# Respacing the weight preparation of the second mixture: sums through the first mixture, splits through the experts

## The chip, the cores and the metric

One core of one Trainium2 chip runs the whole program. The metric is the device time of one execution in microseconds; the kernel before takes 1052.43 us (median of 3 runs, 1051.04 to 1053.65). All other times here are of one execution that the hardware profiler took: 1052.22 us in all, of which 1050.6 us lie between its first and its last instruction (the span).

## The reference

Three stages follow each other, all in float32.

1. Linear attention over 4 batches, 8 heads, 576 positions: features exp(+p) and exp(-p) of projections of q and k, sums of k-features times v, a quotient.
2. A first mixture over the 2304 tokens (512 wide): `h = max(x @ w1, x @ w2, x @ w3)` with 768 hidden columns, then `h @ w_out`.
3. A second mixture with 8 experts: noisy logits choose two experts for each token, and `out[token] += weight * (relu(x @ w1[e]) @ w2[e])`, 1024 hidden columns in each expert.

The kernel writes each operand of most products as a high part (rounded) and a low part (the rest); such a product takes three matmuls, high by high, high by low, low by high.

## The kernel before, in words

**Order.** The kernel writes its order out by hand. `Plan.at(t, f, ...)` records a step with a due time; at the end all steps are sorted by due time and called in that order. The instructions of TensorE (PE), ScalarE (ACT), VectorE (DVE) and SyncE (SP, which issues the direct DMAs) stand in their queues in just that order (`tc.manual_schedule` names these four engines). Each queue is worked off in order and as soon as its waits allow: a due time decides who stands before whom and holds nobody back. GpSimd (POOL) is not in that list. The framework orders its queue by itself; only the routing scatters are tied by hand (`in_order`) to come after the POOL instruction that was recorded before them. The due times of PE's work come from a running `clock[0]`, which `pe(dur, ...)` advances by planned durations: 1.92 us for a group of 12 matmuls with 384 columns (`G1`) and for 9 with 512 columns (`G2`).

**First mixture.** The tokens go through in 6 chunks of 384. A chunk has 6 hidden blocks f. Each has three groups `first(c, f, j)` into three rotating PSUM banks `s`. `larger` frees them: ACT copies the bank of j = 0 into `a`, DVE takes the maximum with the banks of j = 1 and 2 (line 775 and 777). `hidden` splits `a` (ACT writes hh, DVE hl, lines 126 and 127), and `second(c, f)` (line 794) multiplies that by the output weights. Counted in planned us from the start of a chunk (c from 1 to 4; a chunk is 49.08 long): the last `second` of the chunk before stands at 1.92; `second` of block 0 to 4 at 16.44, 24.12, 31.80, 39.48 and 47.16; each has its block's next three groups behind it. `larger` of block 3, j = 0 stands at 28.01, j = 2 at 31.85; the split of the next chunk's input, `split_x`, at 32.30 and `hidden` of block 3 at 32.40; `larger` of block 4, j = 0 at 35.69; `hidden` of block 5 at 47.76. The routing of the chunk before runs beside: its ACT and DVE steps lie at 14.6 to 21.2, and at 22.2 come six scatters on POOL (line 944), each an indirect DMA of `mt` rows to `meta`. `mt` has two buffers, and POOL fills them with token numbers (lines 866 and 867).

**Weight sums.** The experts 2 to 7 (the units with seven products) use a seven-product scheme for the first layer, which needs sums and differences of weight quarters. They are made during the first mixture, in 24 jobs, written out of SBUF into a DRAM tile `sums`, high and low part, and read back much later. A job has four steps: `quarter_load` (SP, two DMAs into a `raw` tile, line 1259), `quarter_sum` (four adds on POOL, lines 1267 to 1270), `quarter_high` (ACT writes `qh`, line 1274), `quarter_out` (DVE writes the low part back into `raw`, line 1279, and SP stores both, line 1281). There are two `raw` tiles in the whole kernel and one `qh` buffer. Six jobs lie in each of the chunks 1 to 4, at 8 + 5.51 i: the third job of a chunk has its load at 19.0, sum at 24.0, high at 27.7, out at 29.2.

**Experts.** A unit is one expert's tokens: unit 0 is expert 0's first 512, unit 1 the next 128 of expert 0, unit n from 2 on expert n - 1 (608 tokens). Units 3 to 8 take the seven products (`seven(n)`). The weights come through a ring of 12 slots, each with a high and a low tile. `refill(i, n, wait)` fetches slots as they come free: `w2_load` (SP into `raw`), `w2_high` (ACT, line 1289), `w2_low` (DVE, line 1297), each at least 3.0 us after the last, `w2_low` 1.2 us behind `w2_high`. A slot that holds a ready sum is loaded from `sums` by two DMAs (line 1292). In unit n `refill` is called after the first layer and after the second. In planned us a unit with seven products takes 21.28 for the first layer and about 28 for the second; unit 2 takes 24.3 and about 28.

The lines of the plan that the change touches:

```python
t = max(clock[0] + wait, split_at[-1] + 3.0)
at(max(split_at[-2] + 0.01, t - 9.0), w2_load, en, en, j)
at(t, w2_high, en, j)
at(t + 1.2, w2_low, en, j)
```

Of the kernel before, what the change touches and what calls it, by code (L numbers as in the profile page):

```python
# [23 lines left out]
class Plan:  # L24
# [5 lines left out]
    def at(self, t, f, *x):  # L30
        self.ops.append((t, len(self.ops), f, x))
# [7 lines left out]
def tile_linear_attention__then__moe__then__noisy_top2_moe(  # L39
# [27 lines left out]
    KD = DM // P  # L67
    F1 = FF1 // P
    F2 = FF2 // P
# [7 lines left out]
    NCHUNK = NT // CT  # L77
# [13 lines left out]
    at = plan.at  # L91
# [967 lines left out]
    ORDER7 = (1, 6, 7, 4, 5, 3, 2)  # L1059

    def seven(n):
        return isinstance(n, int) and n > SEVEN
# [166 lines left out]
    def summed(key, i):  # L1229
        return isinstance(key, int) and key >= SEVEN and i < len(ORDER7) and SEVENTHS[ORDER7[i]][0] == "S"  # L1230
# [68 lines left out]
    def overflow_table():  # L1299
# [12 lines left out]
                "wgn": wgn[one].rearrange("p k e -> p (k e)"),  # L1312
                "cmp": tp.tile([1, MAXO * NREG], F32, name="cmp")}
        used = dict.fromkeys(room, 0)

        def tt(where, *shape):
# [73 lines left out]
    G1 = 3 * KD * CW / 2400   # L1390
    G2 = 3 * CT * DM / 2400
    clock = [T]

    def pe(dur, f, *x):
        at(clock[0], f, *x)
        clock[0] += dur

    def after(d, f, *x):
        at(clock[0] + d, f, *x)

    def first_pe(c, f, j):
        pe(G1, first, c, f, j)
        after(0.05, larger, j)
        if j == 2:
            after(0.6, hidden, c, f)
# [33 lines left out]
    for i in range(2 * 4):  # L1439
        g, j = 1 + i // 4, i % 4  # L1440
        t = END + 0.1 + i * 3.2
# [3 lines left out]
    def finish(c):  # L1445

        for t in range(CT):
            after(0.05 + 0.5 * t, x2_out, c, t)

    def tail(c, i):  # L1450
        if i == 0:
            for t in range(2):
                pe(0.45, x2_turn, c, t)
                after(0.0, x2_in, c, t)
            if c < NCHUNK - 1:
                after(0.1, begin_route, c)
        elif i == 1:
            pe(0.45, x2_turn, c, 2)
            after(0.0, x2_in, c, 2)
        elif i == 2:  # L1460
            pe(1.3, gates, c)
            after(0.0, gates_out, c)
        else:
            pe(0.35, gates_turn, c)
            route_at(c, clock[0])

    split_at = [0.0, 0.0]

    pairs = [(e, j) for e in range(E)
             for j in range(F2 // 2 + (KD if e < SEVEN else len(ORDER7)))]  # L1470

    def base(e):
        return 12 + pairs.index((e, 0))

    def room(i):

        if i < len(pairs):
            after(0.9, w2_room, *pairs[i], i + 12)
            if summed(*pairs[i]):
                after(1.0, w2_high, *pairs[i])  # L1480

    def refill(i, n, wait=0.1, rooms=True):
        for i in range(i, i + n):
            if i >= len(pairs):
                return
            if rooms:
                after(0.0, w2_room, *pairs[i], i + 12)
            if summed(*pairs[i]):
                if rooms:
                    after(1.0, w2_high, *pairs[i])  # L1490
                continue
            en, j = pairs[i]
            t = max(clock[0] + wait, split_at[-1] + 3.0)
            at(max(split_at[-2] + 0.01, t - 9.0), w2_load, en, en, j)
            at(t, w2_high, en, j)
            at(t + 1.2, w2_low, en, j)
            split_at.append(t)

    units = [(0, cap_a, 0), (0, cap_b, E * REGION)] + [(e, cap, e * REGION) for e in range(1, E)]
    jobs = [(e, a, c) for e in range(SEVEN, E) for a in range(2) for c in range(2)]  # L1500
    for c in range(NCHUNK):
        if 0 < c < NCHUNK - 1:
            pitch = (F1 * (3 * G1 + G2) - 13.0) / 6
            for i, job in enumerate(jobs[6 * (c - 1):6 * c]):
                t = clock[0] + 8.0 + pitch * i
                at(t, quarter_load, *job)
                at(t + 5.0, quarter_sum, *job)
                at(t + 8.7, quarter_high, *job)
                at(t + 10.2, quarter_out, *job)
        if c == NCHUNK - 1:  # L1510
            split_at.append(clock[0] + 25.0)
        for f in range(F1):
            for j in range(3):
                if c or f or j > 1:
                    first_pe(c, f, j)
                if c and f == 0 and j == 0:
                    pe(G2, second, c - 1, F1 - 1)
                    finish(c - 1)

                if c and 1 <= 3 * f + j < 5:  # L1520
                    tail(c - 1, 3 * f + j - 1)
            if f in (3, 4) and c + 1 < NCHUNK:
                after(0.5, split_x, c + 1, f - 3)
            if c == NCHUNK - 1 and f == F1 - 1:
                break
            if f:
                pe(G2, second, c, f - 1)
            if c == NCHUNK - 1 and f % 2 == 1:
                refill(2 * f - 2, 3)
            if c == NCHUNK - 1 and f and f % 2 == 0:  # L1530
                refill(2 * f - 1, 1)
    c = NCHUNK - 1
# [12 lines left out]
    finish(c)  # L1545
    split_at.append(clock[0] + 19.0)
    refill(8, 4)

    def open_experts():
# [8 lines left out]
    after(-0.01, open_eh)  # L1558

    for n, (e, M, row0) in enumerate(units):  # L1560
        nsp = 1 if M <= 512 else 2
        cw = M // nsp
        nxt = n + 1 < len(units)
# [5 lines left out]
        if seven(n):  # L1569
            for two in ((0, 1), (2, 3)):  # L1570
                for q_ in ORDER7:
                    for f in two:
                        pe(2 * 3 * HN / 2400, product, n, e, q_, f)
                        d0, d = (-0.03, 0.01) if two[0] and q_ == ORDER7[-1] else (0.02, 0.44)
                        after(d0, sum7, n, q_, f)
                        if q_ in PART7:
                            after(d0 + d, relu7, n, q_, f)
                            after(d0 + 2 * d, low7, n, q_, f)
                    if two[0]:
                        room(base(e) + ORDER7.index(q_))  # L1580
        elif M > P:
            for f in range(F2):
                for s in range(nsp):
                    if n == 0:
                        for i in range(2):
                            pe(d1 / 2, expert1, n, e, M, f, s, cw, range(2 * i, 2 * i + 2))
                            if f < 2:
                                tail(NCHUNK - 1, 2 * f + i)
                    else:
                        pe(d1, expert1, n, e, M, f, s, cw)  # L1590
                    after(0.0, expert_hidden, n, f, s, cw)
                if n == 0 and f == 1:
                    after(0.0, open_experts)
                    tp = clock[0] + 0.01
        else:
            for a in range(2):
                pe(2.56, tile1, n, e, a)
                after(0.0, tile_relu, n, a)
        if seven(n):
            refill(base(e), len(ORDER7), 2.5, False)  # L1600
        elif n:
            refill(base(e), KD, 3.0 if n == 1 else 0.1)
        if n == 4:
# [68 lines left out]
                        turns7(4)  # L1672
                        rows7(2)
        if n:
            refill(base(e) + (len(ORDER7) if seven(n) else KD), F2 // 2)

    ET = mybir.EngineType
    with tc.manual_schedule(engines={ET.PE, ET.Activation, ET.DVE, ET.SP}):
# [55 lines left out]
```

## Time and profile before

| | |
|---|---|
| median of 3 runs | 1052.43 us |
| the profiled execution | 1052.22 us |
| its span | 1050.6 us |
| PE busy (matmul) | 992.9 us, 95% |
| DVE, ACT, POOL busy | 591.3, 448.6, 484.3 us |
| mean granted TensorE clock | 0.978 |
| HBM traffic | 160 GB/s over the span |

Matmuls overlap in the profile, so 95% busy does not mean that nothing can be gained by packing them; but a gap of PE is a gap. The granted clock is the share of full speed (2.4 GHz) that TensorE got in a stretch; it has two levels, 1.0 and 0.5.

In a row of a timeline the columns are: start in us, duration in us, engine, line of the kernel, operation, tiles written and read, shapes, count, and in brackets the idle time of that engine before it and what ended that.

### The profile page before, as it was taken

The page shows a single profiled execution, that of the slowest core. Times are in us where ns is not written, and L with a number is a line of the kernel's source. Part 1 is how long each engine was busy: PE and PEld are TensorE (multiplying, and loading weights), DVE is VectorE, ACT ScalarE, POOL GpSimd, SP SyncE. Part 2 cuts the span into 40 slices and gives each one's busy share as a digit, 9 for nine tenths or more (in the row PEclk, how much of TensorE's full clock was granted, in tenths as well). Part 3 has the DMA queues.
Part 4 walks back from the last instruction along what each step waited for, and adds up shares of the span by engine and source line. Part 5 has one row for each costly group of instructions (what it writes and reads, how often), then busy time and mean ns, then how long its engine had stood idle before and what let it go on. Part 6 is the DMA issues. An engine that isn't in the chain of part 4 may idle for free. (4 is left out here: it accounts for less than half of the span.)

```text
span 1050.6 us, 17138 instructions
## 1 busy us (share of the span) xinstructions
PE 992.9 (95%) x6285; PEld 867.5 (83%) x6285; DVE 591.3 (56%) x1272; ACT 448.6 (43%) x879; POOL 484.3 (46%) x553
## 2 busy tenths in 40 slices
PE   9999999999979978789799999899999999999995
PEld 7777777789978978789689778889888998989893
DVE  5888888874343434434335544365758666666630
ACT  6666666633323224223233523334545464546330
POOL 2677555670243352524404253235556464646261
PEclk9999999999989999899899999999999999999998
DMA  7547765252256353463634443554848393938211
GB/s 192 158 139 182 211 194 169 83 158 64 90 155 216 101 181 131 141 207 84 200 132 121 141 118 126 211 195 145 289 126 303 104 331 104 321 120 315 85 53 43
DMA packets 125351, 169.07 MB, mean 161 GB/s; under 512 B 35630, under 2 KB 86958, under 8 KB 125266
## 3 DMA queue, kind: packets, MB, share of 16 engines
q1 hardware_dynamic: 114338, 138.35, 42.5%
q0 software_dynamic: 10928, 29.62, 8.2%
q8 instruction: 50, 0.82, 0.3%
q14 instruction: 35, 0.29, 0.1%
HBM read 119.38 MB, written 49.14 MB: 160 GB/s over the span
## 5 line engine op out<-in xcount | busy, mean ns | idle before, releaser
L767 PE MATMUL s<-xh,wh 128*128 128x384 f32 x432 | 151.8, 351 | 25.2 <-ACT a L775 25.0
L767 PE MATMUL s<-xl,wh 128*128 128x384 f32 x432 | 148.4, 344 | 0.0
L767 PE MATMUL s<-xh,wl 128*128 128x384 f32 x432 | 148.0, 343 | 0.0
L1225 POOL DMA_INDIRECT out_dram<-o,emeta x40 | 48.1, 1203 | 133.5 <-DVE o L1223 81.1
L767 PEld LDWEIGHTS s<-xh,wh 128*128 128x128 f32 x432 | 83.9, 194 | 30.1 <-ACT a L775 26.7
L1289 ACT ACTIVATE wh<-raw 128x1024 fp32r<-128x1024 f32 x58 | 61.3, 1057 | 61.6 <-DMA raw<-in_moe_w_dram 42.5
L1215 PE MATMUL p<-wh,hh 128*128 128x512 f32 (+1 forms) x216 | 86.4, 400 | 0.0
L1297 DVE TENSOR_TENSOR wl<-raw,wh 128x1024 fp32r<-128x1024 f32 x58 | 70.8, 1220 | 26.6 <-ACT wh L1289 26.6
L1215 PE MATMUL p<-wh,hl 128*128 128x512 f32 (+1 forms) x216 | 85.3, 395 | 0.0
L1215 PE MATMUL p<-wl,hh 128*128 128x512 f32 (+1 forms) x216 | 85.2, 395 | 0.0
L767 PEld LDWEIGHTS s<-xl,wh 128*128 128x128 f32 x432 | 83.9, 194 | 1.5
L777 DVE TENSOR_TENSOR a<-s,a 128x384 f32<-128x384 f32 x72 | 39.8, 553 | 78.4 <-PE s L767 77.9
L767 PEld LDWEIGHTS s<-xh,wl 128*128 128x128 f32 x432 | 83.7, 194 | 0.0
L944 POOL DMA_INDIRECT meta<-mt,si x36 | 36.3, 1008 | 86.0 <-DVE si L940 76.8
L1267 POOL TENSOR_TENSOR raw<-raw 128x256 f32<-128x256 f32 x24 | 18.3, 762 | 122.1 <-DMA raw<-in_moe_w_dram 103.8
L1274 ACT ACTIVATE qh<-raw 128x1024 fp32r<-128x1024 f32 x24 | 25.4, 1060 | 110.7 <-POOL raw L1270 101.9
L1279 DVE TENSOR_TENSOR raw<-raw,qh 128x1024 fp32r<-128x1024 f32 x24 | 30.6, 1273 | 69.6 <-ACT qh L1274 69.2
L480 PE MATMUL k<-vt,kp 128*128 128x128 f32 x512 | 66.4, 278 | 0.1
L480 PEld LDWEIGHTS k<-vt,kp 128*128 128x128 f32 x512 | 60.8, 192 | 6.9 <-issue 6.5
L418 DVE TENSOR_REDUCE m<-p 128x4 f32<-128x512 f32 (+1 forms) x77 | 48.4, 636 | 28.6 <-PE p L408 28.4
L1077 PE MATMUL s<-gx,wh 128*128 128x304 f32 x288 | 62.1, 302 | 0.0
L206 POOL TENSOR_TENSOR nm<-nm,nr 128x512 int32<-128x512 int32 x24 | 30.6, 1274 | 66.6 <-ACT nr L198 35.7
(283 smaller groups left out, 2583.0 us busy)
## 6 DMA issues: line engine op xcount, KB each, us to landing
raw<-in_moe_w_dram SPq DMA_DIRECT2D x58, 512.0 KB, 4.4
raw<-in_moe_w_dram SPq DMA_DIRECT2D x48, 256.0 KB, 3.6
sums<-qh SPq DMA_DIRECT2D x24, 512.0 KB, 3.3
sums<-raw SPq DMA_DIRECT2D x24, 512.0 KB, 4.2
wh<-sums SPq DMA_DIRECT2D x24, 512.0 KB, 6.4
wl<-sums SPq DMA_DIRECT2D x24, 512.0 KB, 8.9
bits<-in_moe_w_dram SPq DMA_DIRECT2D x18, 512.0 KB, 4.3
out_dram<-zrow SPq DMA_DIRECT2D x9, 512.0 KB, 5.2
```

What stands on the lines that cost most here:

```text
L206: nc.gpsimd.tensor_tensor(m_, m_, r_, op=ALU.add)
L418: nc.vector.tensor_reduce(m, st["pj", kind, g][:, :n], axis=AX.X, op=ALU.max, apply_absolute_value=True)
L480: nc.tensor.matmul(st["pkv"][:, 2 * h + sg, :], kp, vv.rearrange("p a d -> p (a d)"), start=(j == 0 and sg == 0), stop=(j == JT and sg == 1))
L767: nc.tensor.matmul(p_, a[:, d, fs], b_, start=(n == 0), stop=(n == 3 * KD - 1))
L777: nc.vector.tensor_tensor(a, p_, st.pop("a"), op=ALU.max)
L944: ins = nc.gpsimd.indirect_dma_start(out=meta, out_offset=bass.IndirectOffsetOnAxis(ap=si[:, t, kk:kk + 1], axis=0), in_=mt[:, t, kk, :], ...
L1077: nc.tensor.matmul(bk["p"], a[:, d, fs], b_[:, d, :], start=(d == 0 and i == 0), stop=(d == 1 and i == 2))
L1215: nc.tensor.matmul(p_, a, b_[:, fw], start=(f == 0 and r == 0), stop=(f == (3 if seven(n) else F2 - 1) and r == 2))
L1225: alone(e, nc.gpsimd.indirect_dma_start(out=out, out_offset=bass.IndirectOffsetOnAxis(ap=mt[:m, i, 1:2], axis=0), in_=o[:m], in_offset=Non ...
L1279: nc.vector.tensor_tensor(lo, t, hi.bitcast(F32), op=ALU.subtract)
L1289: nc.scalar.activation(WE[e, i][0], st["w2", e, i], AF.Copy)
L1297: nc.vector.tensor_tensor(wl, st.pop(("w2", e, i)), wh.bitcast(F32), op=ALU.subtract)
```

## The change

Three things are moved; no instruction of the computation is added or taken away.

1. The 24 sum jobs start together with chunk 1 and follow each other every 8.0 planned us, without regard to chunk borders (chunks 1 to 4 are 196.3 long, the last job's last step is at 195). Sum, high and out come 5.0, 9.5 and 11.0 after the load (before 5.0, 8.7 and 10.2).
2. In `refill` splits follow each other at least 4.5 us apart in units 2 and later (3.0 as before in the last chunk and the units 0 and 1). The low part comes 1.2 us after the high part as before in units 2 and later, and directly behind it before that. In the seven-product units the three splits that are due after the first layer wait 2.5, 7.0 and 17.0 us (before 2.5, 5.5 and 8.5 by their spacing). After unit 1's second layer the refill waits 15.0 us (before 0.1).
3. Ready sums that `refill` loads are spread by 3.0 us each: `wait + 1.0 + 3.0 * (i % 4)` instead of 1.0.

```diff
@@ refill
             if summed(*pairs[i]):
                 if rooms:
-                    after(1.0, w2_high, *pairs[i])
+                    after(wait + 1.0 + 3.0 * (i % 4), w2_high, *pairs[i])
                 continue
             en, j = pairs[i]
-            t = max(clock[0] + wait, split_at[-1] + 3.0)
+            slow = n_now[0] > 1
+            t = max(clock[0] + wait, split_at[-1] + (4.5 if slow else 3.0))
             at(max(split_at[-2] + 0.01, t - 9.0), w2_load, en, en, j)
             at(t, w2_high, en, j)
-            at(t + 1.2, w2_low, en, j)
+            at(t + (1.2 if slow else 0.0), w2_low, en, j)
             split_at.append(t)
@@ first mixture
-        if 0 < c < NCHUNK - 1:
-            pitch = (F1 * (3 * G1 + G2) - 13.0) / 6
-            for i, job in enumerate(jobs[6 * (c - 1):6 * c]):
-                t = clock[0] + 8.0 + pitch * i
+        if c == 1:
+            for i, job in enumerate(jobs):
+                t = clock[0] + 8.0 * i
                 at(t, quarter_load, *job)
                 at(t + 5.0, quarter_sum, *job)
-                at(t + 8.7, quarter_high, *job)
-                at(t + 10.2, quarter_out, *job)
+                at(t + 9.5, quarter_high, *job)
+                at(t + 11.0, quarter_out, *job)
@@ units
+        n_now[0] = n
...
         if seven(n):
-            refill(base(e), len(ORDER7), 2.5, False)
+            own = [i for i in range(base(e), base(e) + len(ORDER7))
+                   if i < len(pairs) and not summed(*pairs[i])]
+            for i, wait in zip(own, (2.5, 7.0, 17.0)):
+                refill(i, 1, wait, False)
...
         if n:
-            refill(base(e) + (len(ORDER7) if seven(n) else KD), F2 // 2)
+            refill(base(e) + (len(ORDER7) if seven(n) else KD), F2 // 2, 15.0 if n == 1 else 0.1)
```

## Rows read from the trace of the kernel before

**Rows 1.** Busy time by stretch: first mixture, experts (window, length, engines, clock, DMA)

```profile
212.40:588.70 376.30, 341.29 (x1823) 314.12 (x1821) 164.64 (x381) 119.67 (x188) 136.63 (x178) 0.95 0.45 141
588.70:1040.10 451.40, 442.45 (x2464) 390.16 (x2462) 255.51 (x535) 195.08 (x412) 219.67 (x248) 1.00 0.54 179
```

**Rows 2.** Who waited for whom, PE alone: total us, times, longest

```profile
PE s L767 <- ACT a L775: 25.0, 4, 7.9
PE p L794 <- ACT hh L126: 9.1, 4, 2.9
PE s L1127 <- DVE hl L1138: 3.9, 1, 3.9
```

**Rows 3.** Busy time by stretch: each stall, to the end of its clock dip

```profile
302.56:311.58 9.02, 3.48 (x11) 3.49 (x12) 3.78 (x5) 3.28 (x5) 6.95 (x10) 0.62 0.55 166
328.80:335.47 6.67, 4.71 (x14) 3.84 (x15) 1.91 (x3) 2.69 (x5) 0.00 (x0) 0.74 0.68 236
368.04:376.43 8.39, 2.85 (x10) 2.85 (x10) 3.14 (x4) 2.69 (x4) 6.93 (x10) 0.80 0.53 157
394.01:400.32 6.31, 3.38 (x8) 2.72 (x9) 2.25 (x3) 2.51 (x5) 0.00 (x0) 0.73 0.54 181
434.03:444.70 10.67, 4.64 (x15) 4.63 (x15) 4.62 (x5) 3.38 (x5) 7.54 (x10) 0.68 0.50 148
461.27:468.59 7.32, 4.41 (x13) 3.49 (x14) 2.25 (x3) 3.28 (x6) 0.00 (x0) 0.77 0.60 208
501.50:512.96 11.46, 3.59 (x12) 3.59 (x12) 3.88 (x5) 2.69 (x4) 7.60 (x10) 0.70 0.46 146
530.17:531.49 1.32, 0.00 (x1) 0.01 (x1) 0.73 (x3) 0.58 (x2) 0.00 (x0) 1.00 1.03 340
668.40:676.80 8.40, 4.49 (x21) 4.49 (x22) 2.84 (x5) 2.42 (x5) 0.00 (x0) 0.80 0.57 213
```

**Rows 4.** Timeline of chunk 1 around its first stall, all engines

```profile
291.93 0.39 PE L794 MATMUL p<-wh,hh 128*128 128x512 f32 x1
292.33 1.25 POOL L944 DMA_INDIRECT meta<-mt,si  x1 [10.02 <-DVE si L940]
...
300.30 0.39 PE L794 MATMUL p<-wh,hh 128*128 128x512 f32 x1
303.17 0.19 POOL L866 COPY mt<-rid 128x6 int32<-128x6 int32 x1 [3.27 <-DMA meta<-mt,si]
306.61 1.06 ACT L1274 ACTIVATE qh<-raw 128x1024 fp32r<-128x1024 f32 x1 [11.97 <-POOL raw L1270]
308.10 0.69 PE L767 MATMUL s<-xh,wh 128*128 128x384 f32 x1 [5.54 <-ACT a L775]
```

**Rows 5.** Timeline of chunk 2: one raw tile from high part to next high part

```profile
372.09 1.06 ACT L1274 ACTIVATE qh<-raw 128x1024 fp32r<-128x1024 f32 x1 [11.97 <-POOL raw L1270]
373.24 1.76 POOL L1268 TENSOR_TENSOR raw<-raw 128x256 f32<-128x256 f32 x1
...
377.64 1.21 SPq L1259 DMA_DIRECT2D raw<-in_moe_w_dram  x2
382.02 0.74 POOL L1267 TENSOR_TENSOR raw<-raw 128x256 f32<-128x256 f32 x1 [4.79 <-DMA raw<-in_moe_w_dram]
385.25 1.06 ACT L1274 ACTIVATE qh<-raw 128x1024 fp32r<-128x1024 f32 x1 [6.55 <-POOL raw L1270]
```

**Rows 6.** Groups of instructions: the two halves of an expert weight's split

```profile
L1289 ACT ACTIVATE wh<-raw 128x1024 fp32r<-128x1024 f32 x58 | 61.3, 1057 | 61.6 <-DMA raw<-in_moe_w_dram 42.5 <-PE p L1215 12.5 <-PE k L1215 6.5
L1297 DVE TENSOR_TENSOR wl<-raw,wh 128x1024 fp32r<-128x1024 f32 x58 | 70.8, 1220 | 26.6 <-ACT wh L1289 26.6
```

**Rows 7.** Timeline of unit 2's start: loads of ready sums, and a late split

```profile
657.54 0.46 SPq L1292 DMA_DIRECT2D wh<-sums  x1
660.49 4.14 SPq L1245 DMA_DIRECT2D raw<-in_moe_w_dram  x2
670.38 1.06 ACT L1289 ACTIVATE wh<-raw 128x1024 fp32r<-128x1024 f32 x1 [6.57 <-DMA raw<-in_moe_w_dram]
```

More of the change, by code (lines that the diff above doesn't have):

```diff
@@ L1473, in base @@
         return 12 + pairs.index((e, 0))
+    n_now = [0]
     def room(i):
```

## The prediction

> **What bounds the kernel now.** I read the busy time by stretch first, then PE's own waits, then one stall after the other on the timeline. PE is busy in 442 of the 451 us of the experts, but only in 341 of the 376 us of the first mixture [rows 1]: what can be gained lies there. The list of PE's waits [rows 2] says where. Four waits on ACT's `a` (25.0 us) and four on ACT's `hh` (9.1 us) are the first mixture's; one wait of 3.9 us is an expert's; no other is over 1.3 us. Rows 3 put them in time: eight stalls, two in each of the chunks 1 to 4, the ones that hold sum jobs. The reader is to see two losses in each row. Length less PE's busy time is the idle time: 5.5, 2.0, 5.5, 2.9, 6.0, 2.9, 7.9 and 1.3, together 34.1 us. The clock column says that a stall brings TensorE down to the lower level, 1.2 of 2.4 GHz, for a while: twice (1 - clock) times the length is the time at half clock, and what of it PE was busy costs half of itself: 1.7, 1.7, 1.4, 1.7, 2.3, 1.7, 1.8 and 0, together 12.4 us. The last, of 1.3 us idle, cost no clock; the next longer one, of 2.0, did. The eight cost 46.5 us. The expert's stall costs 3.9 + 1.7 = 5.6 us in the same way.
>
> Why they come is in rows 4, chunk 1. POOL works in order. It holds six scatters (from 292.33), then a copy into `mt`, whose buffer is free only when the scatters have landed (3.27 us of waiting, 303.17), and only then the third job's sum. ACT, in order too, reaches that job's high part long before, waits 11.97 us for it, and cannot free PSUM banks meanwhile; PE has three banks of slack and then stands 5.54 us. The plan agrees: by due times the high part (27.7) stands just before `larger` of block 3 (28.01); PE can do that block's three groups and needs a bank again at 33.72, which is 9.6 planned us after `second` of block 1. A block of 7.68 planned us takes 300.30 - 291.93 = 8.37 [rows 4], a factor of 1.09: 291.93 + 10.5 = 302.4, and the stall begins at 302.56. I use this ruler below: positions count from `second` of block 1 (planned 24.12), times 1.09.
>
> The second stall of a chunk is the pitch. One `raw` tile goes from high part to next high part in 385.25 - 372.09 = 13.2 us: store, landing, load (377.64), landing, sum (382.02) [rows 5]. Two tiles give a job every 6.6 us; the pitch of 5.51 planned is 6.0 real. The jobs fall behind, and ACT waits for POOL again at the chunk's end.
>
> **The change part by part.**
>
> *Even spacing, in general.* 8.0 planned is 8.7 real, above 6.6: a job's tile is back 2 x 8.7 - 13.2 = 4.2 us before it is due. Where POOL is free, no high part waits. The second stalls lose their cause.
>
> *Even spacing beside the scatters.* The scatters stay at 22.2 in each chunk, and the sum that now follows them in the plan is due at 29.0, 27.9, 26.8 and 25.8 in the chunks 1 to 4, its high part at 33.5, 32.4, 31.3 and 30.3: later for ACT than the 27.7 of before, but drifting forward by 1.08 a chunk. If POOL keeps its order (six scatters, `mt`, sum), that sum ends where it does now, and ACT can start the high part at 306.61 - 291.93 = 14.7 [rows 4] and end at 15.7. What is behind it, by chunk:
> - Chunks 1 and 2: the high part stands behind `hidden` of block 3 (32.40; in chunk 2 by 0.02 only). The next in line is `larger` of block 4, done at about 16.2; PE wants that bank at 41.40, which is 18.8. No stall.
> - Chunk 3: it stands before `split_x` and `hidden` of block 3. ACT does these next; scaled by columns from the 1.06 us of a high part of 1024 columns [rows 4] (768 and 384 columns: 0.8 and 0.5 with some fixed cost) hh is there at 17.1, the low part a us later. PE wants hh at 39.48, or 16.7: a stall of 0.4, and 0.6 more for the low part, 1.0. The job's own low part is now late by 2.4, so its tile returns late: next high part at 14.7 + 13.2 + 2.4 = 30.3. That one (47.34) stands before `hidden` of block 5 (47.76), whose hh then comes at 31.9; PE wants it at 51.0, or 29.3, shifted by the 1.0: stall 1.6.
> - Chunk 4: now the job's low part (31.76) stands on DVE just before `larger` of block 3, j = 2 (31.85). It runs from 15.7 to 16.9 (1.22 us for 1024 columns [rows 6]), the bank is free at 17.5, and PE wants it at 37.56, or 14.65: stall 2.9.
>
> Idle 1.0 + 1.6 + 2.9 = 5.5; two of the three are long enough by rows 3 to cost clock, 1.7 each: 3.4. Remaining: 8.9 of 46.5. Bounds: 0, if the sum comes before `mt` on POOL, since then all this is 3.3 us and more earlier; and 15.2, if the landing takes as long as in chunk 4 of before, whose first stall is 7.9 instead of 5.5 [rows 3]: 2.3 more in chunk 3's first and in chunk 4's stall, and three dips. I take 8.9, because POOL's order was the same in all four chunks: each long stall follows the same chain.
>
> A rule that speaks against spreading the sums: the Trainium skill (GPSIMD Engine Reference, section "8. Key points") says that GpSimd shares its SBUF interfaces with VectorE and contends with DVE instructions that have two SBUF inputs. The trace agrees that this happens: an add of 0.74 us on POOL (382.02) took 1.76 beside DVE's work at 373.24 [rows 5]. By the rule a stuck sum could last 1 to 2 us longer, and the three stalls 3 to 6 in all, so 1012 to 1015. I leave it out of the sum, since DVE stands still too while ACT waits for the stuck sum: the sum is not the one beside busy DVE.
>
> *Low part directly behind the high part (last chunk, units 0 and 1).* Nothing is added, but DVE may now wait for ACT with `larger` and `hidden` queued behind it, and PE behind those. Rows 6 bound it: a high part lasts 1.06 us, so a wait is that long where ACT is on time. PE's three banks cover it. In the other direction the `raw` tile is free about 1.3 us sooner. Between +1.5 and -1.5 us; I take 0. Where ACT itself waits for a load (42.5 us over 58 splits [rows 6]), DVE did so before as well, one instruction later.
>
> *Unit 1's refill 15 us later, sums spread.* In unit 2, ACT waits 6.57 us at 663.8 to 670.4 for a `raw` load (issued behind 660.49), which shared the DMA engines with four loads of ready sums issued from 657.54 [rows 7]. ACT's wait holds `hidden` of the unit, and PE stands 3.9 us [rows 2]. Now that split is due 18 us after unit 1's end, its load 9 us after, and the sums are asked for from 19 us on: load and sums no longer meet, and the load has 9 us instead of the 6 that it lacked. What uses these slots is unit 3, some 50 planned us on. I take the whole 5.6 off; bounds 0 and 5.6.
>
> *Wider spacing in the experts.* Units 3 to 8 have no PE wait above 1.3 us [rows 2], so there is nothing to win beyond about 2 us. Splits come later by up to 8.5 planned us. The tightest: the fourth split after a unit's second layer, at 9.1 planned for the last weight of the next second layer, is wanted at about 24.7: 13 us to spare after its 2.3 us of work [rows 6]. I take 0; bounds -2 and, if queues slip more than that, the last rival.
>
> Sum: 1050.6 - 46.5 + 8.9 - 5.6 = 1007.4 us of span. The profiled execution has 1.6 us around its span (1052.22), and is 0.2 below the median: 1009 us.
>
> **The rivals.**
> 1. *All stalls go.* POOL's framework puts the sum ahead of the `mt` copy, or the sum's data are there earlier: 1050.6 - 46.5 - 5.6 + 1.6 = 1000 us. For it: by the plan the sum's load is up to 3.2 planned us earlier than in chunk 1 against the scatters in chunks 3 and 4. Against: the copy stood first four times out of four.
> 2. *More stays.* The longer landing (15.2 instead of 8.9: 1015), and besides unit 2's stall moves instead of going (+5.6): 1021 us. For it: the wait for the landing was 3.3 us in chunk 1 [rows 4], and chunk 4's longer stall [rows 3] shows that it varies.
> 3. *It doesn't do what it says:* scatters, not spacing, decide, and POOL's chain slips by some 4 us, as much as ACT's high part was moved back. Then the four long stalls stay (25.0 idle and 7.2 of clock) and only the short ones go (9.1 and 5.1): 1050.6 - 14.2 - 5.6 + 1.6 = 1032 us. Against: nothing in the chain is lengthened.
> 4. *Slower:* the wider spacing makes weights late in the experts. Place: the second layer of units 4 to 8, whose last weight has 13 us to spare. From 13 us of slip on PE stands; a slip of 25 costs 12 idle and 1.7 of clock in each of five units, 68 us, and 1077 us in all. For it: ACT and DVE wait for loads there, and each split now has less room behind it. Against: in the experts PE stood once for ACT or DVE [rows 2].
>
> **How the numbers follow.** Forecast (1003 to 1014) 0.47; all stalls gone (996 to 1003) 0.25; more stays (1014 to 1026) 0.17; long stalls stay 0.05; within 0.3% of before 0.02; slower 0.04. Range 996 to 1026: it holds the first three with some loss at the edges, and leaves out the rest. About 0.3%, or 3 us, is what a measurement can tell from no change. Faster 0.94, same 0.02, slower 0.04.
>
> **What would show it.** The changed profile should have no PE wait on `a` or `hh` in chunks 1 and 2; short ones of 1 to 3 us at the ends of chunk 3 and in chunk 4, with ACT's high part waiting for POOL there; POOL's order scatters, copy, sum; no ACT wait of several us for `raw` in unit 2; PE at full pace in units 3 to 8. A long stall in chunk 1 or 2, or a new wait for `wh` or `wl` in the experts, would make the prediction wrong.

## The result and the profile after

The changed kernel takes 998.11 us (median of 4 runs, 997.51 to 999.15) beside 1052.7 us of the kernel before on the same chip (4 runs, 1051.04 to 1053.65): a ratio of 0.948 with an interval of 0.947 to 0.950, 54.6 us less. The forecast was 1009 with a range of 996 to 1026. The sign and the range held; the case that came true is the first rival, "all stalls go, 1000 us", and the likeliest case missed by 11 us.

First the busy time by stretch, cut where the work of the first mixture ends (the columns are those of [rows 1]):

```profile
212.40:542.40 330.00, 327.73 (x1820) 304.18 (x1818) 171.75 (x381) 119.58 (x188) 138.20 (x178) 1.00 0.51 161
542.40:995.90 453.50, 440.33 (x2464) 388.77 (x2462) 255.95 (x534) 196.50 (x412) 215.74 (x248) 0.99 0.53 179
```

The kernel before, cut at the same place and taken to the end of its span:

```profile
212.40:588.60 376.20, 341.19 (x1822) 314.12 (x1821) 164.54 (x381) 119.57 (x188) 136.63 (x178) 0.95 0.45 141
588.60:1050.60 462.00, 442.56 (x2464) 390.16 (x2462) 255.62 (x535) 195.18 (x412) 219.67 (x248) 0.99 0.53 176
```

The first mixture has lost 46.2 us and the rest 8.5. PE is now busy in 327.7 of 330.0 us of the first mixture, at a clock of 1.00: all but 2.3 us of the idle time, and the half clock of [rows 1, 3], are gone. PE's own waits, longest sums first (total us, times, longest), against [rows 2]:

```profile
PE t L822 <- DVE x2l L127: 1.4, 2, 1.0
PE k L589 <- DVE warm L565: 1.3, 1, 1.3
PE t L1016 <- DMA gx<-x2d,emeta: 0.7, 1, 0.7
PE t L918 <- DVE ohs L909: 0.6, 1, 0.6
```

No wait on `a`, `hh` or `hl` of several us is left. The helpers are a different matter. ACT's high parts still wait for POOL's sums, 44.3 us in 13 waits, the longest 6.5:

```profile
ACT qh L1274 <- POOL raw L1270: 44.3, 13, 6.5
```

PE doesn't notice, as chunk 1 shows (timeline of the changed kernel; compare [rows 4]):

```profile
291.64 0.39 PE L794 MATMUL p<-wh,hh 128*128 128x512 f32 x1
...
292.35 1.25 POOL L944 DMA_INDIRECT meta<-mt,si  x1 [3.83 <-DVE si L940]
...
299.60 0.96 POOL L944 DMA_INDIRECT meta<-mt,si  x1 [0.30 <-issue]
...
304.34 0.19 POOL L866 COPY mt<-rid 128x6 int32<-128x6 int32 x1 [3.78 <-DMA meta<-mt,si]
...
307.06 0.74 POOL L1270 TENSOR_TENSOR raw<-raw 128x256 f32<-128x256 f32 x1
...
307.83 1.07 ACT L1274 ACTIVATE qh<-raw 128x1024 fp32r<-128x1024 f32 x1 [6.50 <-POOL raw L1270]
...
308.93 1.58 DVE L1279 TENSOR_TENSOR raw<-raw,qh 128x1024 fp32r<-128x1024 f32 x1 [6.83 <-ACT qh L1274]
...
309.51 1.60 POOL L1269 TENSOR_TENSOR raw<-raw 128x256 f32<-128x256 f32 x1
```

The order scatters, `mt` copy, sum is that of before, and the stuck sum is no earlier: its high part starts 307.83 - 291.64 = 16.2 us after `second` of block 1, against 14.7 in [rows 4]. ACT waits 6.50 us instead of 11.97, and PE works through the whole of 303 to 313. What differs is only what stands behind the high part.

In chunk 3 POOL's order is another (timeline):

```profile
402.69 1.00 POOL L944 DMA_INDIRECT meta<-mt,si  x1 [2.66 <-DVE si L940]
...
409.52 0.96 POOL L944 DMA_INDIRECT meta<-mt,si  x1 [0.30 <-issue]
...
410.51 0.74 POOL L1267 TENSOR_TENSOR raw<-raw 128x256 f32<-128x256 f32 x1
...
413.74 1.06 ACT L1274 ACTIVATE qh<-raw 128x1024 fp32r<-128x1024 f32 x1 [6.00 <-POOL raw L1270]
...
416.17 0.41 POOL L866 COPY mt<-rid 128x6 int32<-128x6 int32 x1 [2.46 <-DMA meta<-mt,si]
```

The sum runs directly behind the sixth scatter, and the copy, which has to wait for the landing, comes after it. In chunk 4 three of the sum's four adds stand even before the scatters (the third at 456.29), and the copy again last:

```profile
456.29 0.74 POOL L1269 TENSOR_TENSOR raw<-raw 128x256 f32<-128x256 f32 x1
...
457.33 1.00 POOL L944 DMA_INDIRECT meta<-mt,si  x1 [0.31 <-DVE si L940]
...
464.94 0.75 POOL L1270 TENSOR_TENSOR raw<-raw 128x256 f32<-128x256 f32 x1
...
465.72 1.06 ACT L1274 ACTIVATE qh<-raw 128x1024 fp32r<-128x1024 f32 x1 [3.83 <-POOL raw L1270]
...
467.06 1.02 POOL L866 COPY mt<-rid 128x6 int32<-128x6 int32 x1 [1.38 <-DMA meta<-mt,si]
```

These are the chunks in which the forecast left stalls, 8.9 us in all, because it took the order of before for granted. How fast the jobs go can be read from the high parts as a group (shortest, median and longest in ns, then the first and the last start):

```profile
L1274 ACT ACTIVATE qh<-raw x24: 1046/1062/1067, 275.5 to 479.5; 128x1024 fp32r<-128x1024 f32 x24
```

23 distances in 479.5 - 275.5 = 204.0 us are 8.87 us per job; planned were 8.0 x 1.09 = 8.7.

### The profile page after: what moved, and what is told of

Same layout as the page of the kernel before. It is cut to its first block, busy times and chain, and to the rows that moved or that the text cites. A ratio compares the mean times of both kernels' runs of the same rounds, so it can differ in the third digit from the quotient of the medians.

```text
span 995.9 us, 17150 instructions
## 1 busy us (share of the span) xinstructions
PE 978.0 (98%) x6285; PEld 856.9 (86%) x6285; DVE 599.4 (60%) x1272; ACT 449.8 (45%) x879; POOL 482.1 (48%) x553
## 5 line engine op out<-in xcount | busy, mean ns | idle before, releaser
L767 PE MATMUL s<-xh,wh 128*128 128x384 f32 x432 | 147.6, 342 | 0.3 <-DVE a L777 0.3
L767 PE MATMUL s<-xh,wl 128*128 128x384 f32 x432 | 145.4, 337 | 0.0
L767 PE MATMUL s<-xl,wh 128*128 128x384 f32 x432 | 145.2, 336 | 0.0
L767 PEld LDWEIGHTS s<-xh,wh 128*128 128x128 f32 x432 | 81.1, 188 | 3.5 <-issue 0.9
L767 PEld LDWEIGHTS s<-xl,wh 128*128 128x128 f32 x432 | 81.2, 188 | 1.5
L767 PEld LDWEIGHTS s<-xh,wl 128*128 128x128 f32 x432 | 81.1, 188 | 0.0
L127 DVE TENSOR_TENSOR gx<-t,gx 128x512 fp32r<-128x512 f32 (+3 forms) x82 | 39.5, 496 | 34.0 <-ACT gx L126 33.8
L126 ACT ACTIVATE gx<-t 128x512 fp32r<-128x512 f32 (+3 forms) x82 | 34.9, 448 | 45.7 <-DVE t L1052 27.9
```

Of the source, the lines that this page charges most:

```text
L126: nc.scalar.activation(hi, src, AF.Copy)
L127: nc.vector.tensor_tensor(lo, src, hi.bitcast(F32), op=ALU.subtract)
L767: nc.tensor.matmul(p_, a[:, d, fs], b_, start=(n == 0), stop=(n == 3 * KD - 1))
```

## The experiments

All times are medians beside the kernel before, which had medians of 1048.3 (experiments 1 to 4), 1048.8 (5 to 8) and 1050.3 us (9 to 12). The ratio is to that.

**1. The jobs' spacing alone**, in the kernel before.

```diff
-        if 0 < c < NCHUNK - 1:
-            pitch = (F1 * (3 * G1 + G2) - 13.0) / 6
-            for i, job in enumerate(jobs[6 * (c - 1):6 * c]):
-                t = clock[0] + 8.0 + pitch * i
+        if c == 1:
+            for i, job in enumerate(jobs):
+                t = clock[0] + 8.0 * i
...
-                at(t + 8.7, quarter_high, *job)
-                at(t + 10.2, quarter_out, *job)
+                at(t + 9.5, quarter_high, *job)
+                at(t + 11.0, quarter_out, *job)
```

> Only the 24 sum jobs are respaced (8.0 apart from chunk 1 on, sum, high and out at 5.0, 9.5, 11.0); refill is that of before. If the eight stalls of chunks 1 to 4 were the jobs' alone, they all go: 46 to 49 us less than before, 1003 to 1007 us, and unit 2's stall of 3.9 us with its clock dip is still there. Rival: part of the gain in the first mixture came from the low part being queued directly behind the high part or from less DMA traffic; then this kernel gains under 40 us (over 1012).

Measured: 1007.34 us (1006.89 to 1009.13), ratio 0.961 (0.958 to 0.963), 41.0 us less, where 46 to 49 were expected. (The kernel before had a median of 1048.3 us here; the execution in which the stalls were counted took 1052.2.) The first mixture has no wait over 0.7 us. Unit 2's stall is still there, and longer than in [rows 2] (PE's waits):

```profile
PE s L1127 <- DVE hl L1138: 5.7, 1, 5.7
```

The clock fell while PE stood. PE went on at 628.01, and the clock was 0.51 in the 3.99 us from there, in which PE was busy throughout: half of that, 2.0 us, on top of the 5.7, together 7.7. The spacing of the jobs alone removes all eight stalls of the first mixture, and leaves unit 2's dearer than it was.

**2. The refills alone** (parts 2 and 3 of the change, without the jobs' lines).

```diff
-            t = max(clock[0] + wait, split_at[-1] + 3.0)
+            slow = n_now[0] > 1
+            t = max(clock[0] + wait, split_at[-1] + (4.5 if slow else 3.0))
...
-            refill(base(e) + (len(ORDER7) if seven(n) else KD), F2 // 2)
+            refill(base(e) + (len(ORDER7) if seven(n) else KD), F2 // 2, 15.0 if n == 1 else 0.1)
```

> Only refill is changed (unit 1's wait, spread sums, wider spacing in units 2 and later, low part directly behind high part before); the sum jobs are those of before. If its only effect is unit 2's stall: 5.6 us less, 1046 to 1048 us, eight stalls of the first mixture as before. Rival: the wider spacing in the experts helps by itself: 8 us or more, 1044 or less. Other rival: no gain, since the stall of unit 2 only moves: 1052.

Measured: 1041.92 us (1041.09 to 1042.55), ratio 0.993 (0.991 to 0.996), 6.4 us less: between the 5.6 expected and the 8 of the rival. PE's waits show the eight stalls of [rows 2] nearly as they were, and no wait in unit 2:

```profile
PE s L767 <- ACT a L775: 22.7, 4, 6.0
PE p L794 <- ACT hh L126: 8.0, 4, 3.5
```

The two parts act on different stalls. Together they give a little more than their sum (41.0 + 6.4 = 47.4, against 50.9 in experiment 5). Some 2 us of that is unit 2's stall, 7.7 instead of 5.6 us in experiment 1; why it is longer there is not shown, as in experiment 3, where the first mixture runs through as well, it is 3.9 again.

**3. Unit 1's wait and the spread of the ready sums undone**, in the changed kernel.

```diff
-                    after(wait + 1.0 + 3.0 * (i % 4), w2_high, *pairs[i])
+                    after(1.0, w2_high, *pairs[i])
...
-            refill(base(e) + (len(ORDER7) if seven(n) else KD), F2 // 2, 15.0 if n == 1 else 0.1)
+            refill(base(e) + (len(ORDER7) if seven(n) else KD), F2 // 2)
```

> The changed kernel with two edits undone: unit 1's last refill waits 0.1 us again instead of 15, and ready sums are asked for at 1.0 us without the 3.0 us spread. If the stall of unit 2 comes from these loads meeting there, it is back: about 5.6 us more than the changed kernel, 1003 to 1005 us, with ACT waiting some 6 us for a raw load early in unit 2. Rival: the stall went because the low parts of units 0 and 1 are queued directly behind the high parts, so that raw tiles come free sooner: then 998 to 1000 us and no stall.

Measured: 1003.93 us (1002.67 to 1005.66), ratio 0.957 (0.954 to 0.959), some 6 us more than the changed kernel. The stall is back at its old size in PE's waits,

```profile
PE s L1127 <- DVE hl L1138: 3.9, 1, 3.9
```

and on the timeline ACT stands for a weight load as in [rows 7]:

```profile
623.05 1.06 ACT L1289 ACTIVATE wh<-raw 128x1024 fp32r<-128x1024 f32 x1 [5.75 <-DMA raw<-in_moe_w_dram]
```

So these two lines, and not the wider spacing of all units, remove unit 2's stall. Which of the two it is was not separated, and neither was whether the load came late because it shared the DMA engines or because it was issued late.

**4. POOL's order forced to that of before**: the `mt` copy tied directly behind the scatters, every sum behind it.

```diff
+        if c + 2 < NCHUNK:
+            fill_mt(c + 2, True)
...
-        nc.gpsimd.tensor_tensor(a22, a21, a22, op=ALU.add)
+        in_order(nc.gpsimd.tensor_tensor(a22, a21, a22, op=ALU.add))
```

> The changed kernel with POOL's order tied by hand: the copy into mt for the chunk after next stands directly behind the scatters, and each weight sum comes after the POOL instruction recorded before it, so that in all of chunks 1 to 4 POOL does scatters, copy, sum. If the order sum before copy in chunks 3 and 4 is what kept them free of stalls, the forecast's working comes true: stalls of about 1.0 and 1.6 us in chunk 3 and 2.9 us in chunk 4 with two clock dips, about 9 us more than the changed kernel, 1004 to 1009 us. Rival: ACT and PE had more slack than the forecast's ruler gave them, and the order does not matter: 998 to 1000 us, no PE gap above 1 us.

Measured: 1004.62 us (1004.03 to 1007.89), ratio 0.959 (0.956 to 0.961); its span is 1002.5, 6.6 more than the changed kernel's. The timeline of chunk 3 and chunk 4 (in this kernel line 956 is the scatter, 859 the copy, 1284 a sum's last add, 1288 the high part):

```profile
408.05 0.97 POOL L956 DMA_INDIRECT meta<-mt,si  x1 [0.30 <-issue]
...
414.03 0.19 POOL L859 COPY mt<-rid 128x6 int32<-128x6 int32 x1 [5.01 <-DMA meta<-mt,si]
...
417.51 1.06 ACT L1288 ACTIVATE qh<-raw 128x1024 fp32r<-128x1024 f32 x1 [11.25 <-POOL raw L1284]
...
419.77 0.50 PE L794 MATMUL p<-wh,hh 128*128 128x512 f32 x1 [1.56 <-ACT hh L126]
...
421.64 0.80 PE L794 MATMUL p<-wh,hl 128*128 128x512 f32 x1 [1.14 <-DVE hl L127]
...
474.36 1.06 ACT L1288 ACTIVATE qh<-raw 128x1024 fp32r<-128x1024 f32 x1 [8.02 <-POOL raw L1284]
...
477.45 0.44 PE L767 MATMUL s<-xh,wh 128*128 128x384 f32 x1 [1.21 <-DVE a L777]
```

With the copy first, ACT's wait in chunk 3 grows from 6.00 to 11.25 us, and PE stands for `hh` and then for `hl` of block 3, where the working had it, but for longer (1.56 + 1.14 for its 0.4 + 0.6). The clock is 0.83 over 410 to 430, which is 6.8 us at half; PE stands for 1.0 us of them, so they cost (6.8 - 1.0) / 2 = 2.9 us. Chunk 4's stall is 1.21 for its 2.9 and costs no clock; the one at the end of chunk 3 (its 1.6) doesn't come. In all 3.9 + 2.9 = 6.8 us, for the 8.9 of the forecast.

**5. The changed kernel again**, unedited, to stand beside 6 to 8.

> The changed kernel itself, to stand beside the other runs of this call. Expected 0.947 to 0.950 of the kernel before.

Measured: 997.86 us (995.95 to 998.48), ratio 0.950 (0.947 to 0.953).

**6. The experts' spacing narrow again**, in the changed kernel.

```diff
-            t = max(clock[0] + wait, split_at[-1] + (4.5 if slow else 3.0))
+            t = max(clock[0] + wait, split_at[-1] + 3.0)
...
-            for i, wait in zip(own, (2.5, 7.0, 17.0)):
+            for i, wait in zip(own, (2.5, 2.5, 2.5)):
```

> The changed kernel with the spacing of splits in the experts undone: 3.0 us apart everywhere, and the three splits after the first layer of a seven-product unit due at 2.5 us and 3.0 apart (2.5, 5.5, 8.5). If the wider spacing is worth nothing, as forecast: within 2 us of the changed kernel. Rival: wider spacing is what the last 2 to 3 us of the gain in the experts came from (PE gaps before transposes and products of units 3 to 8): then 2 to 4 us more than the changed kernel.

**7. The low part 1.2 us late everywhere**, in the changed kernel.

```diff
-            at(t + (1.2 if slow else 0.0), w2_low, en, j)
+            at(t + 1.2, w2_low, en, j)
```

> The changed kernel with the low part 1.2 us behind the high part everywhere, also in the last chunk and the units 0 and 1. If queueing the low part directly behind the high part is worth nothing: within 1.5 us of the changed kernel. Rival: it is what frees raw tiles sooner and takes ACT's waits for loads away at the start of the experts: 2 to 5 us more.

Measured: 999.11 us (997.52 to 1000.81) for 6, and 998.94 (998.01 to 1000.28) for 7; ratio 0.952 (0.949 to 0.955) for both. Against experiment 5 that is 1.3 and 1.1 us, within overlapping intervals. Neither edit is worth anything that can be told from nothing.

**8 and 9. The pitch of the jobs**, in the changed kernel: 5.51 (the old one, but without regard to chunk borders), and 7.0.

```diff
-                t = clock[0] + 8.0 * i
+                t = clock[0] + 5.51 * i
```

> The changed kernel with jobs 5.51 us apart instead of 8.0 (the pitch of before), continuous from chunk 1 on, the same offsets inside a job. 5.51 planned are 6.0 real, and two raw tiles allow a job every 6.6 us. If the pitch against the tile's way round is a cause of stalls by itself, the jobs fall behind by more with each one and ACT waits for POOL at every job: PE stalls of 2 us and more outside the scatters' stretch, 10 to 30 us more than the changed kernel. Rival: only the place of a job beside the scatters matters and ACT's waits are covered by PE's three banks: within 5 us of the changed kernel.

> The changed kernel with jobs 7.0 us apart instead of 8.0 (7.6 real). The run with 5.51 took 196 us from the first high part to the last, 8.5 us for each of 23 steps, scatters included; the way round one raw tile of the kernel before gives 6.6 us. If the whole chain with its scatters sets the pace (8.5), 7.0 is too tight and each job falls 0.9 us behind: PE loses about 15 to 25 us, 1012 to 1024 us. Rival: the tile's way round sets it (6.6), as the forecast had it: 7.0 is wide enough, 997 to 1001 us.

Measured: 1046.83 us (1044.68 to 1047.95), ratio 0.997 (0.995 to 0.999), at 5.51; 1014.61 (1011.74 to 1015.96), ratio 0.966 (0.964 to 0.969), at 7.0. Nearly the whole gain hangs on the pitch; at 5.51 the loss of 49 us is well over the 10 to 30 expected. The high parts as a group, at 5.51, and ACT's wait for POOL's sums before them:

```profile
L1274 ACT ACTIVATE qh<-raw x24: 1052/1059/1066, 275.7 to 472.0; 128x1024 fp32r<-128x1024 f32 x24
```

```profile
ACT qh L1274 <- POOL raw L1270: 90.8, 17, 13.1
```

and at 7.0:

```profile
L1274 ACT ACTIVATE qh<-raw x24: 1052/1062/1066, 274.9 to 473.4; 128x1024 fp32r<-128x1024 f32 x24
```

Planned were 6.0 and 7.6 real us per job; measured are 196.3 / 23 = 8.5 and 198.5 / 23 = 8.6. These distances contain PE's own stalls, since a job's steps stand between PE's in the queues of ACT and DVE; they are a pace of the chain only where ACT waits for the chain. At 5.51 it does so before 17 of the 24 high parts: there the chain has a pace of its own, about 8.5 us with the scatters counted in. ACT's and DVE's queues have one order, so PE is held to that pace as well, and its stalls are spread over all its waits:

```profile
PE s L767 <- ACT a L775: 9.5, 3, 6.3
PE t L808 <- DVE x2l L127: 9.5, 2, 5.5
PE p L794 <- ACT hh L126: 8.6, 4, 4.8
PE t L918 <- DVE ohs L909: 5.9, 3, 2.5
PE p L794 <- DVE hl L127: 2.1, 3, 1.2
```

The lag adds up: 196.3 - 23 x 6.0 = 58 us at 5.51, of which PE pays 49 (1046.8 - 997.9); the rest, 9 us, may be what its banks cover.

At 7.0 PE pays 17 us, and mostly elsewhere (PE's waits):

```profile
PE p L794 <- DVE hl L127: 4.0, 2, 2.0
PE s L767 <- DVE a L777: 3.9, 1, 3.9
PE t L918 <- DVE ohs L909: 3.2, 2, 1.7
PE p L794 <- ACT hh L126: 2.3, 2, 1.2
```

All but the 3.2 us for `ohs` come within 9 us behind the `mt` copy: `hh` and `hl` of block 3 in chunks 1 and 2, the bank of j = 2 in chunk 3. In this kernel POOL has the copy ahead of the sum in all four chunks (copy at 303.25, 364.05, 425.40 and 483.98), and by due times the high part beside the scatters stands at 30.5, 30.4 and 30.3 in the chunks 1 to 3, before `hidden` of block 3 (32.40), in chunk 3 also the low part at 31.84 before `larger` of j = 2 (31.85). These are the places that the prediction worked out for copy first. So the loss at 7.0 is at least in part one of place and order beside the scatters; how much of it is pace, no run separates.

**10 and 11. `mt` with five buffers**, so that the copy waits for no landing in chunks 2 to 4, in the kernel before (10) and in the changed one (11). Six chunks need six copies, so the sixth still waits for scatters to land, in chunk 1: 2.81 us before 301.95 in experiment 10, 4.46 before 306.42 in experiment 11.

```diff
-        mt = small([P, CT, 2, 3], "mt", I32)
+        mt = small([P, CT, 2, 3], "mt", I32, bufs=5)
```

> The kernel before with five mt buffers instead of two, so that the copy into mt never waits for scatters to land. If the 3.3 us of that wait are part of the long stalls, each of the four shrinks by about 3.3 us (5.5 to some 2 us): 10 to 15 us less than before, 1034 to 1040 us. Rival: the pitch alone decides, PE is slaved to the chain of jobs and gets the time back as a stall elsewhere in the chunk: 1044 to 1050 us.

> The changed kernel with five mt buffers. ACT's waits of some 6 us for POOL in chunks 1 and 2 should fall to about 2 us. Since PE's banks cover them already, the time stays: 996 to 999 us. Rival: the shorter chain also takes the last small PE gaps away: 995 or less.

Measured: 1044.98 us (1042.09 to 1048.04), ratio 0.996 (0.994 to 0.998), and 997.58 (996.96 to 999.49), ratio 0.950 (0.947 to 0.953). In the kernel before, three of the four long stalls shrink to some 2.1 us, while chunk 1's, whose copy still waits, stays at 5.0, and the ones at the chunks' ends, 2.0, 2.9, 2.9 and 1.3 in [rows 3], become 1.4, 4.6, 3.5 and 3.5 (PE's waits):

```profile
PE p L794 <- ACT hh L126: 13.5, 5, 4.6
PE s L767 <- ACT a L775: 11.3, 4, 5.0
PE s L1127 <- DVE hl L1138: 5.1, 1, 5.1
```

Taking the landing out of the way in three chunks is worth 5 us by itself, as the rival had it, and not the 10 to 15 expected: what is saved at the scatters is mostly paid again at the chunk's end, since at the old pitch the chain is late anyway. In the changed kernel it is worth nothing, since no stall hangs on it: ACT's wait in chunk 2 falls from 6.36 to 2.81 us, the one in chunk 1, whose copy still waits, is 7.21, and PE notices neither.

**12. The old offsets of high part and store**, in the changed kernel.

```diff
-                at(t + 9.5, quarter_high, *job)
-                at(t + 11.0, quarter_out, *job)
+                at(t + 8.7, quarter_high, *job)
+                at(t + 10.2, quarter_out, *job)
```

> The changed kernel with the old places inside a job: high part 8.7 and out 10.2 after the load instead of 9.5 and 11.0. By the ruler of the forecast the high part beside the scatters then stands before the next chunk's input split and before hidden of block 3 in chunk 2 too (31.6 against 32.3 and 32.4): a stall of about 1 us there and at most one clock dip, 999 to 1002 us. Rival: 0.8 us is nothing to a queue that waits anyway: 997 to 999 us.

Measured: 997.78 us (996.52 to 998.62), ratio 0.950 (0.947 to 0.953): no stall, also not in chunk 2, where the prediction counted 0.02 planned us between the high part and `hidden`. The later offsets are worth nothing that can be told. But those 0.02 us were not put to the test: in this kernel POOL has the sum ahead of the copy in chunk 2 too (sixth scatter at 355.67, the adds from 356.64, the copy at 361.28), although no due time of a POOL step was changed.

## Why the prediction was right where it was, and wrong by 11 us

- **The eight stalls are the loss, 46.5 us.** Right. The first mixture is 46.2 us shorter (376.2 - 330.0), at a clock of 1.00, and experiment 1 alone brings 41.0 of run time while its unit 2's stall is dearer by 2.1 (7.7 for 5.6).
- **Chunks 1 and 2: ACT waits, PE doesn't.** Right, by the mechanism named: the high part starts no earlier (16.2 us after `second` of block 1, for 14.7 before) and ACT waits 6.50 us (6.36 in chunk 2), but what stands behind the high part is not wanted yet.
- **"If POOL keeps its order (six scatters, `mt`, sum)": the step that failed.** The 8.9 us that were left in chunks 3 and 4 rest on "POOL's order was the same in all four chunks". The changed profile has the sum ahead of the copy in both. Experiment 4 ties POOL to the old order and brings 6.6 us of span back, with stalls and clock of 6.8 us in the places that the working gave for chunk 3's first and chunk 4's; experiment 9, where POOL kept the old order by itself, has stalls in the same places. So the working behind the order was right in its places and, to 2 us, in its sum, but not in its terms (idle 2.7, 0 and 1.2 us for 1.0, 1.6 and 2.9): that the sum comes so near is partly luck. The order was wrong. The prediction's own ruler pointed there: the sum's due time moves forward against the scatters by 1.08 a chunk, and four chunks of before, in which it never moves, are one observation and not four. What rule the framework uses to order POOL's queue was not measured (in experiment 12 the order changed in chunk 2 without a change to POOL's due times); the chance of .25 for this rival was too low.
- **"Two tiles give a job every 6.6 us", 4.2 us to spare per tile.** Too generous, and hidden by the result. The 13.2 us of [rows 5] are a round with POOL free, and the working prices the scatters for the job beside them, not for those that have to catch up. Six jobs of 6.6 us and the time for which scatters and copy hold POOL, 292.35 to 304.34 in chunk 1, or 12.0 us, make 51.6 us a chunk, 8.6 per job: an estimate from these rows that agrees with the 8.5 of experiment 8. By it the planned 8.7 leaves 0.1 to 0.2 us per job, not 2.1 per job or 4.2 per tile. That 8.0 planned us were just enough is luck as far as the working goes. The 17 us lost at 7.0 don't decide here, as they can also come from the place beside the scatters.
- **The long landing as an upper bound (rival 2), the scatters as the cause (rival 3).** Neither came. Experiment 10 takes the landing out of three of the four chunks of the kernel before and gains 5 us of the 46, and experiment 8 loses nearly all of the gain by the old pitch alone: this speaks against scatters and pitch as two causes with a stall each, and for one chain that is too slow for its plan.
- **A stuck sum is not lengthened.** Right: its adds took 0.73 to 0.74 us up to 307.06. The Trainium skill (GPSIMD Engine Reference, section "8. Key points") says that GpSimd shares its SBUF interfaces with VectorE and contends with DVE instructions that have two SBUF inputs. The next lines of the same timeline agree: the following sum's add at 309.51 took 1.60 us and the low part on DVE at 308.93 took 1.58, beside each other, for 0.74 and 1.22 alone [rows 5, 6]. It meets the sum behind the stuck one, whose end ACT doesn't wait for here (high part at 312.11). In chunk 3 an add of the sum behind took 1.73 us (417.00) and ACT waited 4.88 for its end, without a stall of PE.
- **Unit 2: 5.6 us off.** Right in size, a little small: 6.4 by experiment 2, 6 by experiment 3. The mechanism fits the changed profile, in which the loads of ready sums are issued from 624.56 on and ACT's splits at 621.80, 625.16 and 633.55 wait for no load; that the sharing of the DMA engines was the reason is not shown by itself. Of the 8.5 us by which the experts and the end are shorter, some 2 to 3 are small waits that no run singles out.
- **Low part and wider spacing: 0.** Right to within some 1 us (experiments 6 and 7), and so rival 4 had nothing to start from.

The sum of the prediction with 8.9 put to 0 is 1000 us, and 997 with the larger gain in the experts. The range held because the first rival came true, not because the likeliest case did.

## What to carry to other kernels

A chain of helpers whose steps stand in in-order queues between the steps of the bounding engine has a pace of its own; measure it with everything that shares its queues (here 8.5 us per job at the tight pitch, not the 6.6 of an undisturbed round), and space the chain just above that: at 8.0, 7.0 and 5.51 planned us the same work took 998, 1015 and 1047 us. A wait of 6 us on a helper costs nothing as long as what is queued behind it is not wanted yet, so look at the order behind the wait before its length. Where an edit moves due times and one queue is ordered by the framework, take that queue's order as unknown and give both orders their price.

## What was not expected of the hardware

Stalls of nearly the same length differ in what they cost of TensorE's clock. Three stalls of one execution, each with some us behind it (busy time by stretch of experiment 10; the clock is the third number from the end):

```profile
365.15:374.00 8.85, 6.79 (x38) 6.73 (x39) 4.54 (x6) 3.83 (x6) 4.29 (x5) 1.00 0.66 200
429.21:437.00 7.79, 5.62 (x33) 5.62 (x33) 4.13 (x5) 2.69 (x4) 4.07 (x5) 1.00 0.62 204
492.32:501.00 8.68, 6.59 (x30) 6.59 (x30) 3.58 (x5) 2.94 (x5) 3.60 (x5) 0.80 0.55 181
```

Their idle time (length less PE's busy time) is 2.06, 2.17 and 2.09 us, and only the last brought the clock down, which cost (1 - 0.80) x 8.68 = 1.7 us. In experiment 8 single stalls of 2.27 and 2.45 us kept the full clock too, while one of 1.87 us in experiment 2 lost it (0.77 over the 7.58 us from 526.42). So the prediction's reading that 1.3 us costs no clock and 2.0 does is not a limit: a stall of about 2 us has to be priced as a chance. The Trainium skill (TensorE: Matmul & The Clock Gate, section "What's actually happening") says that the activity monitor's window runs freely and is not reset when a kernel starts; these rows don't contradict that, as equal stalls at different moments fell differently; that the moment decides, and not the work around a stall, no run here shows.

The time of the kernel with stalls also varies more from run to run: 1046.1 to 1055.5 us in 16 runs of the kernel before, 996.0 to 998.5 in 6 of the changed one. That the clock's share of it is the reason was not tested.
